# Another order for the first four tiles of an adaLN block: the second tile's k in two parts, two quarters of w_mod straight to TensorE, four more low parts by DMA

## The chip, the cores and the metric

One core of one Trainium2 chip runs the kernel. The engines are TensorE (PE, with its weight loads PEld), VectorE (DVE), ScalarE (ACT), GpSimd (POOL) and SyncE (SP), which here only issues DMAs. Each engine works through its own list of instructions in order and waits on semaphores for what the others make. The metric is the device time of one execution in microseconds (us); the smaller, the better.

## The reference

A block on 2048 tokens of 448 channels, all in float32. Six vectors of modulation come from `c`; two residual branches follow, a linear attention over 16 heads of 28 channels and an MLP across the tokens:

```python
mod = (_silu(c) @ w_mod).reshape(c.shape[0], 6, 1, -1)     # sa, ca, ga, sb, cb, gb
h = _layernorm(x, axis=-1) * (1 + ca) + sa
x = x + ga * _A_ref(h, A_wqkv, A_wo)      # phi(q), phi(k): where(t > 0, t + 1, exp(t)) + 1e-6
h = _layernorm(x, axis=-1) * (1 + cb) + sb
x = x + gb * _B_ref(h, B_w1, B_b1, B_w2, B_b2)   # layernorm, w1 over tokens, gelu, w2 over tokens
```

The attention is linear: kv is the sum over all tokens of the outer product of phi(k) and v, z the sum of phi(k), and each token's output is phi(q) kv / (phi(q) z), then `wo`.

## The kernel before, in words

**Precision.** PE multiplies quickly in the format float32r. An operand is cut into a high part (a copy to float32r, on ACT) and a low part (full minus high), and a product takes three matmuls: high by high, high by low, low by high. The cut `split` (lines 78 to 80) has ACT write the high part and DVE subtract. In a second way (`w_low_dma`, and `split_to` for pieces listed in `PIECE_DMA`) ACT writes the negated high part and a DMA issued by POOL adds the full operand to it in memory.

**Tiles.** The 2048 tokens are 16 tiles of 128 rows. 448 channels are four chunks of 128, where the fourth chunk holds the last 64 channels twice, so that high and low part go through one matmul. A projection (`project`, lines 333 to 347) of one tile onto k or q is 11 matmuls. Tile 0 is the exception: `project0` multiplies the raw float32 weights in 4 slower matmuls, so that it needs no split weights.

**The front (lines 495 to 577).** The order is written out by hand, engine by engine; what an engine meets first in this list it does first. `load_mod` brings four quarters of w_mod for each modulation vector. `mod_acc` (ACT) scales the first quarter by silu(c), `mod_add` (DVE) adds quarters 1, 2 and 3. `col_sum(j)` sums the rows with small matmuls against ones, to have scale and bias of tile 0 as columns: for the first two chunks it takes the accumulation before its last quarter (`part`) and that last quarter directly against `scb`, ones times silu(c); for the other chunks it takes the complete accumulation. `mod_sum` sums the complete accumulation into all rows, and `mod_out` copies it from PSUM to SBUF on ACT.

For a tile t, `a_stats` (DVE, with a power on POOL) gives mean and deviation, `a_norm_a` and `a_norm_b` (DVE) the modulated layernorm h, `a_dup` (ACT) the doubled last chunk, `a_transpose` (PE) turns h, and `a_split` (ACT, DVE) cuts it into `hh` and `hl`. `w_high` (ACT) and `w_low` (DVE) cut wqkv's chunks into `wh` and `wl`. Then k of tile 0, 1, 2 and q of tile 0, 1, 2 are projected; `a_exp` (ACT) and `a_pk` (DVE) make phi(k), `a_phi_q` phi(q), `a_pk_parts` cuts phi(k), and `a_high` cuts h for the outer product. In the order before, k of tile 1 (`project(1, 1, "kp", True)`, all 11 matmuls) stands ahead of q of tile 0, and the low parts of wqkv's k chunks ahead of tile 2's layernorm.

**The loop (lines 581 to 635).** For t from 3 to 15: k of tile t, transposes of t + 1, the outer product of tile t - 3 (`a_outer`, 11 matmuls into four banks), and at t = 3 and 4 also q of tile t.

**The stage after it (lines 840 to 904).** Iteration i transposes `pn` of tile i (phi(q) over its denominator), multiplies by kv and wo (`b_out`), computes the second layernorm for older tiles, and multiplies 12 matmuls of the first group of w1 for tile i - 5 (`step`). DVE makes `pn` (L729, L737) from a sum that POOL raises by 1e-6 (`den`, L722). At the end of an iteration `split_to(10 + (i + 1) // 2)` cuts the next piece of w1 (128 by 512): pieces 10 to 13 in iterations 1, 3, 5 and 7, pieces 14 to 17 in 9, 11, 13 and 15. The rest of the kernel is the MLP: PE with the remaining pieces of w1, gelu, and w2.

**Buffers.** Eight PSUM banks, 76 slots in SBUF for most tiles; a new tile waits until the readers of the tile before it in the same slot are done.

Of the kernel before, what the change touches and what calls it, by code (L numbers as in the profile page):

```python
# [8 lines left out]
F32 = mybir.dt.float32  # L9
# [5 lines left out]
P = 128  # L15
# [3 lines left out]
G = 112  # L19
# [1 line left out]
DH = 28  # L21
EPS = 1e-5

PIECE_DMA = (14, 15, 16, 17)
PRE_LOAD = {12: 2, 13: 4, 14: 6, 15: 8}
KV_LAG = 3
Q_EARLY = (3, 4)
# [20 lines left out]
def block_kernel(ctx: ExitStack, tc: tile.TileContext, x, wqkv, wo, w1, b1, w2, b2, c, wmod, out):  # L48
# [16 lines left out]
    def slot(name, w=D, dt=F32, parts=P):  # L65
        return slots.tile([parts, w], dt, name=name, tag="slot", padded_shape=[P, 512])
# [92 lines left out]
    def mod_out(j, ps):  # L159
        mods[j] = cst.tile([P, D], F32, name=f"mod{j}")  # L160
        nc.scalar.activation(mods[j], ps[:, :D], AF.Copy, bias=1.0 if j in (1, 4) else 0.0)
# [5 lines left out]

    def mod_add(j, k):
        acc = macc[j]
        if k == 3:  # L170
            part[j] = acc
            macc[j] = slot(f"acc{j}_3", parts=G)
        nc.vector.scalar_tensor_tensor(macc[j], wm[j, k], sc[:, k:k + 1], acc, op0=ALU.mult, op1=ALU.add)

    def mod_part(j, k):
# [33 lines left out]
    def w_low(j, ch):  # L209
        w, r = Whi[j, ch], raw_w[j, ch]  # L210
        if ch < 3:
            Wlo[j, ch] = moving(tslot, f"wl{j}_{ch}")
            nc.vector.tensor_sub(Wlo[j, ch], r, w.bitcast(F32))
        else:
            nc.vector.tensor_sub(w[64:128], r[64:128], w[64:128].bitcast(F32))  # L215

    def w_low_dma(j, ch):
        w, r = Whi[j, ch], raw_w[j, ch]
        if ch < 3:
            Wlo[j, ch] = moving(tslot, f"wl{j}_{ch}")  # L220
            lo, hi = Wlo[j, ch], w
        else:
            lo = hi = w[64:128]
            r = r[64:128]
        nc.scalar.activation(lo, hi.bitcast(F32), AF.Copy, scale=-1.0)
        nc.gpsimd.dma_start(lo, r, accum_op=ALU.add)
# [78 lines left out]
    def a_norm_a(t):  # L305
        h = slot(f"h{t}", 512)
        nc.vector.scalar_tensor_tensor(h[:, :D], X[t], st[t][0], mods[1],
                                       op0=ALU.add if t in ACT_STATS else ALU.subtract, op1=ALU.mult)
        hs[t] = h

    def a_norm_b(t, sa=None):
        h = hs[t]
        nc.vector.scalar_tensor_tensor(h[:, :D], h[:, :D], st.pop(t)[1], mods[0] if sa is None else sa,
                                       op0=ALU.mult, op1=ALU.add)

    def a_dup(t):
        nc.scalar.activation(hs[t][:, D:], hs[t][:, 384:D], AF.Copy)
# [3 lines left out]
    def a_transpose(t):  # L321
        h = hs[t]
        tps[t] = bank(f"tp{t}")
        for ch in range(4):
            nc.tensor.transpose(tps[t][:, ch * P:(ch + 1) * P], h[:, ch * P:(ch + 1) * P], ident)  # L325

    def a_split(t):
# [2 lines left out]
        split(tps.pop(t), hh, hl)  # L330
        heads[t] = (hh, hl)

    def project(t, j, name, late_low=False):
        hh, hl = heads[t]
        ps = bank(f"{name}{t}")
        o = ps[:, :D]
        todo = []
        for ch in range(4):
            a, b = (hh, ch, Whi[j, ch]), (hl, ch, Whi[j, ch])
            todo += [a, b] if ch == 3 else [a, (hh, ch, Wlo[j, ch]), b]  # L340
        if late_low:
            ws = [Wlo[j, ch] for ch in range(3)]
            key = lambda m: 3 if m[1] == 3 else 2 if any(m[2] is w for w in ws) else 0 if m[0] is hh else 1
            todo.sort(key=key)
        for n, (a, ch, b) in enumerate(todo):
            nc.tensor.matmul(o, a[:, ch * P:(ch + 1) * P], b, start=(n == 0), stop=(n == 10))  # L346
        return o
# [3 lines left out]
    def a_exp(t, ps):  # L351
        eks[t] = (slot(f"ek{t}"), slot(f"rk{t}"))
        nc.scalar.activation(eks[t][0], ps, AF.Exp)
        nc.scalar.activation(eks[t][1], ps, AF.Relu)
# [56 lines left out]
    def a_pk(t, ps):  # L411
        pkf[t] = phi_k(t, ps, tslot if t < 2 else slot)
# [30 lines left out]
                nc.tensor.matmul(cacc[ch][:, :D], a[:, s], b, start=(t == 0 and i == 0),  # L443
                                 stop=(t == NT - 1 and i == len(todo) - 1))

    scb = cst.tile([G, 64], F32, name="scb")

    h0t = slot("h0t", 512)
    raw_t = {}
# [7 lines left out]
    def col_sum(j):  # L457
        at = 0 if j else 4

        todo = [(part[j], ones[:G, :64], (0, 1)), (wm[j, 3], scb, (0, 1)), (macc[j], ones[:G, :64], (2, 3))]  # L460
        for n, (a, b, chunks) in enumerate(todo):
            for c in chunks:
                ps = colq if j == 0 and c < 2 else colp
                nc.tensor.matmul(ps[:, 64 * (at + c):64 * (at + c + 1)], a[:, CH[c][0]:CH[c][1]], b,
                                 start=(n == c == 0), stop=True, skip_group_check=True)
        groups = ((0, 0, 2, (0, 1)), (0, 2, 3, (2,)), (64, 3, 4, (3,))) if j == 0 else ((0, 0, 3, ()), (64, 3, 4, ()))
        for p0, c0, c1, mod in groups:
            ps = colq if j == 0 and c0 < 2 else colp
            nc.scalar.activation(cols[p0:, at + c0:at + c1], ps[p0:, 64 * (at + c0):64 * (at + c1 - 1) + 1:64], AF.Copy,
                                 bias=float(j))  # L470
            for ch in mod:
                if j == 0 and ch in MOD_ACT:
                    a_mod(ch)
# [14 lines left out]
    def project0(j, name, between):  # L488
        ps = bank(f"{name}0")
        for ch in range(4):  # L490
            nc.tensor.matmul(ps[:, :D], h0t[:, ch * P:(ch + 1) * P], raw_t[j][ch], start=(ch == 0), stop=(ch == 3))  # L491
            between.get(ch, int)()
        return ps[:, :D]

    raw_t = {j: [raw_w[j, ch] for ch in range(4)] for j in (0, 1)}
    a_stats(0)
    nc.vector.tensor_scalar_mul(scb, ones[:G, :64], sc[:, 3:4])
    mod_acc(1)
    nc.scalar.activation(ones_r, ones, AF.Copy)
    mod_acc(0)  # L500
# [23 lines left out]
    a_stats(2)  # L524
    a_split(1)
    w_high(1, 2)
    w_low(1, 1)
    w_high(1, 3)
    w_high(0, 0)
    w_low_dma(0, 0)  # L530
    w_low(1, 2)
    w_low(1, 3)
    mod_out(0, sap)
    a_norm_a(2)
    kp1 = project(1, 1, "kp", True)
    for ch in range(1, 4):
        w_high(0, ch)
    a_norm_b(2)
    a_dup(2)
    a_exp(0, kp0)  # L540
    w_low(0, 1)
    a_stats(3)
    a_pk(0, kp0)
    qps[0] = project0(0, "qp", {1: lambda: a_transpose(2)})
    a_split(2)
    a_norm_a(3)
    a_exp(1, kp1)
    a_high_act(1)
    a_norm_b(3)
    a_dup(3)  # L550
    w_low(0, 2)
    w_low(0, 3)
    a_stats(4)
    a_norm_a(0)
    a_norm_b(0)
    kp2 = project(2, 1, "kp")
    a_high(0)
    a_pk(1, kp1)
    a_transpose(3)
    qps[1] = project(1, 0, "qp", True)  # L560
    del heads[1]
    a_split(3)
    a_norm_a(4)
    a_norm_b(4)
    a_phi_q(1)
    a_high_low(1)
    a_exp(2, kp2)
    a_pk_parts(0)
    a_pk(2, kp2)
    a_phi_q()  # L570
    a_dup(4)
    a_pk_parts(1)
    a_q(2)
    a_high(2)
    a_stats(5)
    a_high(3)
    a_phi_q()
    load_mod(2)
    wo_sb = []
    late = [t for t in range(KV_LAG, NT) if t not in Q_EARLY]  # L580
    for t in range(3, NT):
        kp = project(t, 1, "kp")
        if t + 1 < NT:
            a_transpose(t + 1)
        a_outer(t - KV_LAG)
        if t in Q_EARLY:
            a_q(t)
        if t == 10:
            mp = mod_sum2(2)
        if t + 1 < NT:  # L590
            a_split(t + 1)
        if t + 2 < NT:
            a_norm_a(t + 2)

        for j, i in MOD_AT.get(t, ()):
            mod_part(j, i)
        if 11 <= t < 15:
            nc.vector.tensor_mul(wo_sb[t - 11], wo_sb[t - 11], mods[2][:G])
        a_exp(t, kp)
        if t + 2 < NT:  # L600
            a_norm_b(t + 2)
        a_pk(t, kp)
        a_phi_q()
        a_pk_parts(t - 1)
        if t + 3 < NT:
            a_stats(t + 3)
        if t + 2 < NT:
            a_dup(t + 2)
        if t == 3:
            a_high(4)  # L610
        if t + 2 < NT:
            a_high(t + 2)
        if t == 10:
            mod_out(2, mp)
        if t + 4 < NT:
            load_x(t + 4)
        if 5 <= t < 9:
            mod_part(2, t - 5)
        if t == 9:
            mod_split(2)  # L620
        if 5 <= t <= 5 + QLATE:
            phi_q_sum(t - 5)
        if t in (10, 11):
            load_mod(14 - t)
        if t == 4:
            for g in range(4):
                w = tslot(f"wo{g}", parts=G)
                nc.sync.dma_start(w, wo[g * G:(g + 1) * G, :])
                wo_sb.append(w)
            load_qkv(2, tslot)  # L630
            b1c = cst.tile([P, NF], F32, name="b1c")
            nc.sync.dma_start(b1c, b1.rearrange("(k p) -> p k", p=P))
            b2c = cst.tile([P, NT], F32, name="b2c")
            nc.sync.dma_start(b2c, b2.rearrange("(k p) -> p k", p=P))
        load_to(PRE_LOAD.get(t, 0))
# [562 lines left out]
```

## Time and profile before

| | us |
|---|---|
| median of 3 runs (lowest, highest) | 441.48 (441.41, 441.74) |
| span of the profiled execution | 440.0 |
| PE busy | 434.6 |
| DVE busy | 367.4 |
| ACT busy | 265.0 |
| POOL busy | 118.4 |

The span runs from the first to the last instruction of one profiled execution; the runs' time has 1.48 us more around it. In a timeline a row is a group of like instructions in order: start, time from the first start to the last end, engine, line, operation, `out<-in` by the names above, count, and in brackets how long the engine sat idle and what ended that. In the chain of work that ended last a row is start, time and what. Matmuls are pipelined: the next starts before the one before it has ended, so start to start is the time that one takes of PE.

### The profile page before, as it was taken

The numbers are of one execution on the slowest core, as the hardware profiler recorded it, in microseconds if no ns is written. First come the engines' busy times: TensorE is split into PE (matmuls) and PEld (weight loads), VectorE is DVE, ScalarE is ACT, GpSimd is POOL, SyncE is SP. The second block draws the span as 40 slices with busy tenths as digits, with TensorE's granted clock in tenths as the row PEclk, the third lists the DMA queues.
The fourth block names the chain that finished last, engine by engine and source line by source line (L and its number), as shares of the span: only waits on it lengthen the run. The fifth ranks groups of instructions, "written<-read, shape, count | busy, mean of one in ns | idle before, by whom it ended". The sixth has DMA issues, their size and how long they took to land.

```text
span 440.0 us, 7266 instructions
## 1 busy us (share of the span) xinstructions
PE 434.6 (99%) x2390; PEld 402.4 (91%) x2390; DVE 367.4 (84%) x795; ACT 265.0 (60%) x566; POOL 118.4 (27%) x192
## 2 busy tenths in 40 slices
PE   8999999999999999999999999999999999999996
PEld 7689999999899999999999999999999999999996
DVE  5997897978899999997469586439999988898894
ACT  3868977755646676777666254236675555655550
POOL 2205675520014456564300000010111320231110
PEclk9999999999999999999999999999999999999999
DMA  8987999993430004222417555476667977986531
GB/s 235 292 225 113 172 198 236 220 254 99 134 85 2 24 25 120 50 51 52 140 60 238 162 162 176 135 192 184 155 150 189 181 168 177 185 165 194 86 52 34
DMA packets 64446, 63.47 MB, mean 144 GB/s; under 512 B 8408, under 2 KB 56728, under 8 KB 64408
## 3 DMA queue, kind: packets, MB, share of 16 engines
q1 hardware_dynamic: 54608, 47.62, 36.6%
q0 software_dynamic: 9792, 15.37, 22.3%
q8 instruction: 19, 0.31, 0.3%
q14 instruction: 19, 0.16, 0.1%
q10 hardware_dynamic: 8, 0.00, 0.0%
HBM read 41.88 MB, written 7.34 MB: 112 GB/s over the span
## 4 chain that ended last, share of the span: by engine, by line
PE 95%; DMA 3%; DVE 1%; SPq 0%; issue 0%; DVEq 0%
PE y L1014 19%; PE up L815 10%; PE up L814 10%; PE up L816 10%; PE y L1015 9%; PE op L764 8%; PE cacc L443 8%; PE qp L346 8%; PE kp L346 7%; DMA wr<-in_A_wqkv_dram 2%; PE tq L744 2%; PE tp L325 1%; DMA wm<-in_w_mod_dram 1%; PE kvb L677 1%; PE qp L491 1%; PE wp L832 1%
## 5 line engine op out<-in xcount | busy, mean ns | idle before, releaser
L815 PE MATMUL up<-h2l,ph 128*128 128x448 f32 x224 | 81.3, 363 | 0.0
L814 PE MATMUL up<-h2h,ph 128*128 128x448 f32 x224 | 81.2, 362 | 0.0
L816 PE MATMUL up<-h2h,pl 128*128 128x448 f32 x224 | 80.7, 360 | 0.0
L974 POOL DMA_DIRECT2D a<-a x16 | 14.1, 965 | 145.9 <-DVE u L931 75.9
L814 PEld LDWEIGHTS up<-h2h,ph 128*128 128x128 f32 x224 | 42.0, 188 | 3.3
L80 DVE TENSOR_TENSOR pl<-pr,ph 128x512 fp32r<-128x512 f32 x52 | 35.1, 685 | 11.5 <-ACT ph L79 8.6
L816 PEld LDWEIGHTS up<-h2h,pl 128*128 128x128 f32 x224 | 41.9, 187 | 3.0
L815 PEld LDWEIGHTS up<-h2l,ph 128*128 128x128 f32 x224 | 42.0, 188 | 2.2
L79 ACT ACTIVATE ph<-pr 128x512 fp32r<-128x512 f32 x52 | 31.6, 628 | 17.8 <-PE up L815 11.8
L1036 ACT ACTIVATE cc<-y 128x448 f32<-128x448 f32 x24 | 13.0, 544 | 22.6 <-PE y L1015 22.6
L443 PE MATMUL cacc<-pkh,xh 128*128 128x448 f32 x64 | 24.3, 379 | 0.0
L443 PE MATMUL cacc<-pkl,xh 128*128 128x448 f32 x64 | 23.2, 363 | 0.0
L764 PE MATMUL op<-oh,pth 128*128 128x448 f32 x60 | 23.0, 383 | 0.0
L346 PE MATMUL kp<-wh,hh 128*128 128x448 f32 x60 | 22.2, 375 | 0.2 <-DVE wh L215 0.2
L1057 POOL DMA_DIRECT2D out_dram<-yt x14 | 12.7, 910 | 34.5 <-DVE yt L1043 25.0
L764 PE MATMUL op<-oh,ptl 128*128 128x448 f32 x60 | 21.7, 362 | 0.0
L346 PE MATMUL qp<-wh,hh 128*128 128x448 f32 x60 | 21.6, 365 | 0.0
L346 PE MATMUL kp<-wh,hl 128*128 128x448 f32 x60 | 21.6, 365 | 0.0
L346 PE MATMUL qp<-wh,hl 128*128 128x448 f32 x60 | 21.4, 362 | 0.0
L722 POOL TENSOR_SCALAR den<-den 128x16 f32<-128x16 f32 x16 | 8.8, 549 | 43.0 <-DVE den L719 43.0
L302 POOL TENSOR_TENSOR rs<-ve,mhalf 128x1 f32<-128x1 f32 x16 | 14.6, 915 | 19.0 <-DVE ve L300 18.1
L931 DVE TENSOR_TENSOR u<-u,mod 128x448 f32<-128x448 f32 x14 | 8.7, 619 | 11.9 <-ACT u L930 11.6
(228 smaller groups left out, 1347.4 us busy)
## 6 DMA issues: line engine op xcount, KB each, us to landing
pr<-in_B_w_dram SPq DMA_DIRECT2D x56, 256.0 KB, 3.1
a<-in_B_w_dram SPq DMA_DIRECT2D x32, 256.0 KB, 4.7
a<-in_B_w_dram SPq DMA_DIRECT2D x32, 192.0 KB, 4.6
wm<-in_w_mod_dram SPq DMA_DIRECT2D x24, 196.0 KB, 4.2
x<-in_A_x_dram SPq DMA_DIRECT2D x16, 224.0 KB, 3.9
out_dram<-x SPq DMA_DIRECT2D x14, 224.0 KB, 2.0
out_dram<-yt POOLq DMA_DIRECT2D x14, 224.0 KB, 4.7
pk<-pk POOLq DMA_DIRECT2D x12, 224.0 KB, 4.6
```

The costliest lines, as they stand in the source:

```text
L79: nc.scalar.activation(hi, full, AF.Copy)
L80: nc.vector.tensor_sub(lo, full, hi.bitcast(F32))
L302: nc.gpsimd.tensor_tensor(rs, ve, mhalf[:, 0:1], op=ALU.pow)
L346: nc.tensor.matmul(o, a[:, ch * P:(ch + 1) * P], b, start=(n == 0), stop=(n == 10))
L443: nc.tensor.matmul(cacc[ch][:, :D], a[:, s], b, start=(t == 0 and i == 0), stop=(t == NT - 1 and i == len(todo) - 1))
L764: nc.tensor.matmul(opb[t][:, :D], a[:, g * P:(g + 1) * P], b, start=(n == 0), stop=(n == len(todo) - 1))
L814: nc.tensor.matmul(ps[:, :D], hi[:, sl], mh, start=first, stop=False)
L815: nc.tensor.matmul(ps[:, :D], hi[:, sl], ml, start=False, stop=False)
L816: nc.tensor.matmul(ps[:, :D], lo[:, sl], mh, start=False, stop=last)
L974: nc.gpsimd.dma_start(w, a, accum_op=ALU.add)
L1014: nc.tensor.matmul(ps[:, :D], h[:, s], w, start=opens and r == r0, stop=False, skip_group_check=True)
L1015: nc.tensor.matmul(ps[:, :HD], l[:, s], wh, start=False, stop=closes and r == PAIRS - 1 - (LAST if (q, m) == (NP - 1, 6) else 0), skip_gro ...
```

## The change

Four things change. `PIECE_DMA` grows from pieces 14 to 17 to pieces 10 to 17: four more pieces of w1 get their low part from ACT and a POOL DMA instead of a DVE subtraction. For modulation vector 0, `part` is the accumulation before quarter 2, and quarters 2 and 3 go directly to TensorE, each against its own scaled ones (`scb` is a pair now): two more column sums. k of tile 1 comes in two calls: the six products with the weights' high parts of chunks 0 to 2 ahead of q of tile 0, the three with their low parts and the two of chunk 3 behind it. And the instructions of the front stand in another order: tile 2's layernorm, which reads `sap` from PSUM, ahead of the low parts of k's chunks; exp and phi(k) of tile 0 behind the third tile's work; k of tile 2 ahead of q of tile 1 and its preparation; part of the high cut and phi(q) of tiles 2 and 3 moved into the loop's first turn.

```diff
-PIECE_DMA = (14, 15, 16, 17)
+PIECE_DMA = tuple(range(10, 18))
...
-        if k == 3:
+        if k == (3 if j else 2):
             part[j] = acc
-            macc[j] = slot(f"acc{j}_3", parts=G)
+            macc[j] = slot(f"acc{j}_{k}", parts=G)
...
+    def products(t, j, late):
+        hh, hl = heads[t]
+        if not late:
+            return [(a, ch, Whi[j, ch]) for a in (hh, hl) for ch in range(3)]
+        return [(hh, ch, Wlo[j, ch]) for ch in range(3)] + [(a, 3, Whi[j, 3]) for a in (hh, hl)]
+
+    def project_some(o, todo, first, last):
+        for n, (a, ch, b) in enumerate(todo):
+            nc.tensor.matmul(o, a[:, ch * P:(ch + 1) * P], b, start=(first and n == 0), stop=(last and n == len(todo) - 1))
...
-    scb = cst.tile([G, 64], F32, name="scb")
+    scb = {k: cst.tile([G, 64], F32, name=f"scb{k}") for k in (2, 3)}
...
-        todo = [(part[j], ones[:G, :64], (0, 1)), (wm[j, 3], scb, (0, 1)), (macc[j], ones[:G, :64], (2, 3))]
+        todo = [(part[j], ones[:G, :64], (0, 1))] + [(wm[j, k], scb[k], (0, 1)) for k in range(3 if j else 2, 4)]
+        todo.append((macc[j], ones[:G, :64], (2, 3)))
...
-    nc.vector.tensor_scalar_mul(scb, ones[:G, :64], sc[:, 3:4])
+    for k in scb:
+        nc.vector.tensor_scalar_mul(scb[k], ones[:G, :64], sc[:, k:k + 1])
...
     a_split(1)
     w_high(1, 2)
-    w_low(1, 1)
     w_high(1, 3)
     w_high(0, 0)
     w_low_dma(0, 0)
+    a_norm_a(2)
+    kp1 = bank("kp1")[:, :D]
+    project_some(kp1, products(1, 1, False), True, False)
+    a_norm_b(2, sap[:, :D])
+    mod_out(0, sap)
+    a_dup(2)
+    w_low(1, 1)
     w_low(1, 2)
     w_low(1, 3)
-    mod_out(0, sap)
-    a_norm_a(2)
-    kp1 = project(1, 1, "kp", True)
     for ch in range(1, 4):
         w_high(0, ch)
-    a_norm_b(2)
-    a_dup(2)
-    a_exp(0, kp0)
+    qps[0] = project0(0, "qp", {1: lambda: a_transpose(2)})
+    project_some(kp1, products(1, 1, True), False, True)
     w_low(0, 1)
     a_stats(3)
-    a_pk(0, kp0)
-    qps[0] = project0(0, "qp", {1: lambda: a_transpose(2)})
     a_split(2)
+    a_exp(0, kp0)
     a_norm_a(3)
-    a_exp(1, kp1)
-    a_high_act(1)
     a_norm_b(3)
     a_dup(3)
+    kp2 = project(2, 1, "kp")
+    a_transpose(3)
+    a_exp(1, kp1)
     w_low(0, 2)
     w_low(0, 3)
+    a_pk(0, kp0)
     a_stats(4)
+    a_split(3)
+    a_pk_parts(0)
+    a_high_act(1)
+    a_phi_q()
+    a_exp(2, kp2)
     a_norm_a(0)
     a_norm_b(0)
-    kp2 = project(2, 1, "kp")
-    a_high(0)
+    a_high_act(0)
+    a_norm_a(4)
+    a_high_low(0)
+    a_norm_b(4)
+    a_dup(4)
     a_pk(1, kp1)
-    a_transpose(3)
     qps[1] = project(1, 0, "qp", True)
     del heads[1]
-    a_split(3)
-    a_norm_a(4)
-    a_norm_b(4)
-    a_phi_q(1)
+    a_phi_q()
     a_high_low(1)
-    a_exp(2, kp2)
-    a_pk_parts(0)
+    a_pk_parts(1)
     a_pk(2, kp2)
-    a_phi_q()
-    a_dup(4)
-    a_pk_parts(1)
     a_q(2)
     a_high(2)
     a_stats(5)
-    a_high(3)
-    a_phi_q()
...
         if t == 3:
+            a_high(3)
             a_high(4)
```

## The prediction

> **What bounds the kernel now.** I read the page first, then the chain of work that ended last, then the timelines of PE, DVE and POOL where the chain shows a piece longer than its kind.
>
> ```profile
> span 440.0 us, 7266 instructions
> PE 434.6 (99%) x2390; PEld 402.4 (91%) x2390; DVE 367.4 (84%) x795; ACT 265.0 (60%) x566; POOL 118.4 (27%) x192
> ```
>
> The span is 440.0 us and the median of the runs 441.48: 1.48 us lie around the span, and I take them as unchanged. PE is busy 99% of the span, so a change in order can win only what PE still loses. The change adds no work to PE but two small column sums. Where PE loses time is read from the chain, where equal pieces should take equal times:
>
> ```profile
> 18.24 0.67 PE kp L346 x2
> 18.91 1.50 PE qp L491 x4
> 20.42 0.44 PE tp L325 x4
> 20.85 1.51 PE qp L491 x4
> 22.36 2.21 PE kp L346 x11
> ...
> 25.01 4.42 PE qp L346 x22
> 29.42 2.47 PE kp L346 x11
> 31.89 0.44 PE tp L325 x4
> 32.33 2.27 PE cacc L443 x11
> 34.60 2.20 PE qp L346 x11
> ...
> 43.86 2.20 PE kp L346 x11
> ...
> 166.91 0.58 PE tq L744 x4
> ...
> 197.40 0.63 PE tq L744 x4
> ```
>
> Eleven products take 2.20 to 2.21, so 0.20 each; the fourth tile's k (29.42) takes 0.26 more, the first outer product (32.33) 0.06 more. Four transposes take 0.44; those at 166.91 and 197.40 take 0.14 and 0.19 more. The largest loss lies where this part of the chain begins:
>
> ```profile
> 10.41 0.66 PE L464 MATMUL colq<-ones,acc 112*128 112x64 f32 x4 [0.42 <-DVE acc L173]
> 10.91 0.61 PE L464 MATMUL colq<-scb,wm 112*128 112x64 f32 x4
> 11.35 0.61 PE L464 MATMUL colp<-ones,acc 112*128 112x64 f32 x4
> ...
> 12.61 1.67 PE L491 MATMUL kp<-wr,h0t 128*128 128x448 f32 x4
> ...
> 17.27 0.79 PE L346 MATMUL kp<-wl,hh 128*128 128x448 f32 x3
> 18.24 0.47 PE L346 MATMUL kp<-wh,hh 128*128 128x448 f32 x1 [0.18 <-DVE wh L215]
> 18.55 0.36 PE L346 MATMUL kp<-wh,hl 128*128 128x448 f32 x1
> ```
>
> The three wl products of the second tile's k start at 17.27 and leave PE free at 17.87. The next starts at 18.24, its successor 0.31 later instead of 0.20: 0.48 lost, waiting for DVE's low part of the last weight chunk (the row names L215). So the early losses are 0.48 + 0.26 + 0.06 = 0.80, the late ones 0.14 + 0.19 = 0.33.
>
> **The change part by part.** The DVE rows that the new order moves:
>
> ```profile
> 8.91 2.19 DVE L173 SCALAR_TENSOR_TENSOR acc<-wm,sc,acc 112x448 f32<-112x448 f32 x3 [0.88 <-DMA wm<-in_w_mod_dram]
> ...
> 15.78 0.68 DVE L80 TENSOR_TENSOR hl<-tp,hh 128x512 fp32r<-128x512 f32 x1
> 16.38 1.15 DVE L213 TENSOR_TENSOR wl<-wr,wh 128x448 fp32r<-128x448 f32 x2
> 17.56 0.62 DVE L215 TENSOR_TENSOR wh<-wr,wh 64x448 fp32r<-64x448 f32 x1
> 18.22 0.69 DVE L307 SCALAR_TENSOR_TENSOR h<-x,mv,mod 128x448 f32<-128x448 f32 x1
> 19.04 0.69 DVE L313 SCALAR_TENSOR_TENSOR h<-h,rs,mod 128x448 f32<-128x448 f32 x1
> 19.64 0.62 DVE L213 TENSOR_TENSOR wl<-wr,wh 128x448 fp32r<-128x448 f32 x1
> ...
> 21.11 0.61 DVE L359 SCALAR_TENSOR_TENSOR pk<-ek,rk 128x448 f32<-128x448 f32 x1
> 21.65 0.68 DVE L80 TENSOR_TENSOR hl<-tp,hh 128x512 fp32r<-128x512 f32 x1
> ```
>
> *Quarters of w_mod.* The sums over chunks 0 and 1 need DVE's accumulation only up to its first add (8.91 + 0.68, about 9.6) instead of the second. PE pays one group more, 0.44 (10.91 to 11.35). PE sat idle for 0.42 before 10.41, so at the latest it is free at 9.99; three groups then end at 11.31. The last group cannot start before the third add is out (8.91 + 2.19 = 11.10, plus the 0.06 between DVE's 18.18 and PE's 18.24), 11.16. It stood at 11.35: k of the first tile starts 0.04 to 0.19 earlier. The second scaled vector of ones is one small DVE instruction in the wait for the same transfers: nothing; uncovered it would be some 0.2.
>
> *Second tile's k in two parts.* The first tile's k and the transposes in it take 3.45 (the pieces at 18.91 to 22.36 have the same shape) from 12.61, to 16.06, so now to 15.87 to 16.02; three hh products bring PE to 16.47 to 16.62. The hl products need DVE's low part of the head (15.78 + 0.68 = 16.46), which does not move: everything ahead of it on DVE stays. I let PE wait for it and pay the 0.11 restart seen between 18.24 and 18.55: 16.52 + 0.11 + 0.60 = 17.23. In the chain's reckoning, which has the next piece 0.16 behind (18.91 for a slot that ends at 18.75), that is 17.39, and q of the first tile starts there instead of at 18.91.
>
> From there the chain's own pieces add up: 1.50 + 0.44 + 1.51 to 20.84; five products of the late part, 1.00, to 21.84; k of the third tile 2.21 to 24.05; transposes 0.44 to 24.49; two q 4.42 to 28.91; k of the fourth tile 2.21 without its wait, to 31.12; transposes to 31.56; outer product 2.21 to 33.77. It was 34.60. **Gain 0.83.**
>
> *What covers it.* DVE: the third tile's normalisation (18.22, 19.04) changes places with three low parts (16.38 to 18.18). It ends near 17.9, and its transposes on PE come at 18.7. The low parts end near 19.6 and are used at 20.7 (0.16 off the chain's 20.84). The next low part then stands at about 19.6, as before. Behind it `pk` (21.11) moves back by several instructions, so the head's low part at 21.65 starts near 21.1 and ends at 21.8. The third product of that k needs it at 22.08: 0.3 of room, the least on DVE. Without it PE waits one for one. The fourth tile's low part then comes about two us before its use, which is where the 0.26 goes.
>
> One covered step is a DMA; ACT is the other engine to watch (timeline of POOL, list of DMA issues with KB and us to landing up to 40 us, timeline of ACT):
>
> ```profile
> 17.68 1.04 POOL L226 DMA_DIRECT2D wl<-wr  x1 [1.19 <-ACT wl L225]
> ...
> xl<-h POOLq DMA_DIRECT2D x2, 192.0 KB, 3.9
> wl<-wr POOLq DMA_DIRECT2D x1, 224.0 KB, 7.3
> ...
> 40.99 0.58 ACT L79 ACTIVATE hh<-tp 128x512 fp32r<-128x512 f32 x1
> ```
>
> The low part of wqkv's first q chunk lands at 17.68 + 7.3 = 25.0. It is used six products into the second tile's q: 24.33 (24.49 less 0.16) + 1.20 = 25.53, with about 0.16 to load: 0.3 to 0.4 of room, where before it had more than a microsecond. ACT gets the third tile's exp and relu of q and the fourth tile's high part and negated copy (about 0.58 each by the row at 40.99) behind the loop's start. The first pair fills a wait for PE; the second comes on top, 1.16. The row at 40.99 hangs on PE's q before it, so 40.99 - 0.83 + 1.16 = 41.3, done at 41.9, and k needs it at 43.86 - 0.83 = 43.0. Covered by 1.1. SP's queue keeps its order; POOL's keeps the layernorms' powers in order and meets one DMA (the fourth tile's cut) later, in the loop's first turn, with its use three tiles on.
>
> *Four more pieces of w1.* Each takes one DVE subtraction away and adds one ACT copy and one POOL DMA (busy time in a stretch, then timelines of DVE and POOL):
>
> ```profile
> 160.00:180.00 20.00, 20.00 (x108) 18.40 (x107) 19.73 (x48) 14.12 (x30) 12.30 (x25) 1.00 0.29 80
> 161.80 0.68 DVE L80 TENSOR_TENSOR pl<-pr,ph 128x512 fp32r<-128x512 f32 x1
> ...
> 173.09 0.95 POOL L257 DMA_DIRECT2D pl<-pr  x1
> ...
> 174.75 0.64 POOL L722 TENSOR_SCALAR den<-den 128x16 f32<-128x16 f32 x1 [0.27 <-DVE den L719]
> ...
> 197.29 0.19 DVE L737 COPY pn<-pn 128x64 f32<-128x64 f32 x1
> ```
>
> In this stage (PE, PEld, DVE, ACT, POOL in the first row) DVE is busy 19.73 of 20: it is bound nearly as tightly as PE, and both late stalls are transposes that wait for its `pn` (the copy at 197.29 ends at 197.48, beside the transposes of 197.40). The subtraction at 161.80, about 0.60 up to DVE's next start, falls away in the iteration before the stall at 166.91. 0.60 is more than 0.14 and 0.19 together, so I take both as gone: **gain 0.33**; 0 if DVE waits for something else there, which keeps the far end. The three earlier pieces I cost at nothing: DVE still had room there. ACT has 6 of 20 us free. POOL's DMA delays what stands behind it by about a microsecond; DMAs of the same kind already run in the later iterations, and there the den instruction (174.75) still waited for DVE, not DVE for POOL.
>
> Sum: 0.83 + 0.33 = 1.16 of the span's 440.0, so 438.8, and 441.48 - 1.16 = **440.3**. Bounds: without the 0.11 restart and with the first tile's earlier start (at most 0.19) in full, 0.30 more, 440.0; with no late gain and the two narrow covers (0.3 each) missed by as much again, 0.6 less in front and 0.33 less behind, 441.25.
>
> **The rivals.** 0.2%, about what a measurement here can tell from no change, is 0.88 us.
>
> *Only the front.* DVE's freed 0.60 ends in a wait on ACT or POOL and the late stalls stay: 441.48 - 0.83 = 440.65, within 0.2%. For it: DVE is in step with both engines there. Against it: the stage's DVE idles for 0.27 in 20 us.
>
> *It does nothing.* The order moves the waits instead of removing them: room of 0.3 in two places, a full ACT. Each of the two may cost 0.3 to 0.5, and what is left of 0.83 is noise: 441.2.
>
> *Slower, by the low part that comes by DMA.* PE stands still until it lands, and nothing can pass it. It now has 0.3 to 0.4 of room. Up to 1.5 late it eats only the gain; from 2.4 late the kernel is slower by 0.2%. If it landed 3.4 later (as much again as its 7.3 exceeds the 3.9 median of the xl transfers nearby), 3.0 would be lost: 441.48 - 1.16 + 3.0 = 443.3. Against it: the same issue, from the same instruction, slightly earlier, and no new transfer beside it.
>
> *Slower, by POOL.* If a piece's DMA held POOL far longer than 0.95 under a full DVE, den behind it would come late. In the iteration of 161.80 it may last about 1.2 before DVE waits, and DVE is about 0.4 ahead of PE after losing its subtraction; past 1.6 each microsecond is PE's, and from 3.3 the kernel is slower by 0.2%. DVE leaves POOL a pause of 0.07 in an iteration of 5 (0.27 in 20); held for a whole iteration, the loss is 3.4: 441.48 - 0.83 + 3.4 = 444.0. Against it: 0.95 in the same stage.
>
> The Trainium skill (SBUF — State Buffer, "SBUF: two separate sides") speaks against this part of the change: GpSimd cannot write a DMA's descriptors while DVE holds the port that the two share; the section after it ("A bandwidth-pool intuition that's wrong (but worth ruling out)") gives about 620 ns alone and 3100 ns beside a DVE copy. By that figure the sum would be 441.48 - 0.83 + 1.5 = 442.15, an estimate; this trace, with 0.95 beside a DVE busy 19.73 of 20, does not show the lock.
>
> **How the numbers follow.** Forecast 0.58; only the front 0.17; nothing 0.10; late DMA 0.09; POOL 0.06. Faster by over 0.2%: 0.58. Within 0.2%: 0.27. Slower: 0.15. The forecast's own range is 439.9 to 440.6. With the next two cases it reaches from 440.0 less 0.07 to 441.25 plus 0.26, by the runs' own spread around their median (441.41 to 441.74): 439.9 to 441.5; the slower cases are left out.
>
> **What would show it.** q of the first tile at about 17.4 in the chain instead of 18.91, with the hl products just behind 16.5; no piece over 2.21 among the k products up to 35 and q of the fourth tile near 33.8; transposes of 0.44 at about 166 and 196.3; POOL's four new DMAs near 0.95 each, and den still waiting for DVE. The prediction is wrong if a k or q product waits for a `wl` or an `hl` between 16 and 32, if the first k of the loop waits for ACT's `hh` near 43, or if the stalls of the `pn` transposes are still there.

## The result and the profile after

The changed kernel takes 440.77 us in the median of 21 runs, the kernel before 441.57 beside it: ratio 0.9983, 95% interval 0.9977 to 0.9988, so 0.75 us faster (0.53 to 1.02). Forecast were 440.3 and a gain of 1.16. The profiled execution's span fell from 440.0 to 439.1.

The page of the changed kernel, busy times, and its chain of work that ended last (start, time, what):

```profile
span 439.1 us, 7288 instructions
PE 433.9 (99%) x2394; PEld 402.4 (92%) x2394; DVE 365.1 (83%) x792; ACT 266.9 (61%) x570; POOL 119.3 (27%) x196
```

```profile
12.51 1.50 PE kp L502 x4
...
17.43 8.12 DMA wl<-wr
25.60 3.48 PE qp L356 x16
29.07 2.20 PE kp L356 x11
...
31.71 2.21 PE cacc L453 x11
33.93 2.20 PE qp L356 x11
...
70.09 2.29 PE cacc L453 x11
...
166.32 0.44 PE tq L758 x4
...
196.68 0.44 PE tq L758 x4
```

The fourth tile's k (29.07) takes 2.20, where it took 2.47; the outer product 2.21, where it took 2.27; both late transposes take 0.44, where they took 0.58 and 0.63. All the losses that the prediction listed are gone. The start of a piece in the chain is 0.16 behind that of the same piece in PE's timeline (12.51 for 12.35), so starts are compared within one of the two. New is the second row: a transfer stands in the chain for 8.12 us, the low part of wqkv's first q chunk. What it costs is seen in PE's timeline of the changed kernel:

```profile
12.35 1.67 PE L502 MATMUL kp<-wr,h0t 128*128 128x448 f32 x4
...
16.41 0.79 PE L341 MATMUL kp<-wh,hl 128*128 128x448 f32 x3
17.04 1.67 PE L502 MATMUL qp<-wr,h0t 128*128 128x448 f32 x4
...
24.75 0.77 PE L356 MATMUL qp<-wh,hl 128*128 128x448 f32 x3
25.60 0.88 PE L356 MATMUL qp<-wl,hh 128*128 128x448 f32 x3
26.31 0.36 PE L356 MATMUL qp<-wh,hh 128*128 128x448 f32 x1
```

Three products at 24.75 and three at 25.35 would end their slots at 25.95; the next stands at 26.31. So 0.36 is lost at the second tile's q: the transfer landed at 17.43 + 8.12 = 25.55, 0.55 later than in the profile before although it was issued 0.25 earlier.

Where the 0.9 of the spans came from: q of the fourth tile stands at 33.93 in the chain instead of 34.60, 0.67. One outer product (70.09) gives 0.08 back. At the transposes of 166.32 the lead is 0.59 (166.91 before); there 0.14 was lost before and is not now, so at 196.68 it is 0.72 (197.40 before), and behind those transposes, where 0.19 was lost before, 0.91.

### The profile page after: what moved, and what is told of

It reads as the page before. It is cut to its first block, busy times and chain, and to the rows that moved or that the text cites. A ratio compares the mean times of both kernels' runs of the same rounds, so it can differ in the third digit from the quotient of the medians.

```text
span 439.1 us, 7288 instructions
## 1 busy us (share of the span) xinstructions
PE 433.9 (99%) x2394; PEld 402.4 (92%) x2394; DVE 365.1 (83%) x792; ACT 266.9 (61%) x570; POOL 119.3 (27%) x196
## 4 chain that ended last, share of the span: by engine, by line
PE 95%; DMA 3%; DVE 1%; ACT 0%; issue 0%; SPq 0%; DVEq 0%
PE y L1028 19%; PE up L829 10%; PE up L828 10%; PE up L830 10%; PE y L1029 9%; PE op L778 8%; PE cacc L453 8%; PE qp L356 7%; PE kp L356 7%; DMA wl<-wr 2%; PE tq L758 2%; PE tp L325 1%; DMA wm<-in_w_mod_dram 1%; PE kvb L691 1%; PE wp L846 1%; PE colp L475 0%
## 5 line engine op out<-in xcount | busy, mean ns | idle before, releaser
L80 DVE TENSOR_TENSOR pl<-pr,ph 128x512 fp32r<-128x512 f32 x48 | 32.3, 686 | 11.5 <-ACT ph L79 8.6
L79 ACT ACTIVATE ph<-pr 128x512 fp32r<-128x512 f32 x48 | 29.1, 627 | 17.8 <-PE up L829 7.4
L453 PE MATMUL cacc<-pkh,xh 128*128 128x448 f32 x64 | 24.3, 379 | 0.0
L356 PE MATMUL qp<-wh,hl 128*128 128x448 f32 x60 | 21.4, 362 | 0.0
L356 PE MATMUL kp<-wh,hl 128*128 128x448 f32 x56 | 20.3, 363 | 0.0
L356 PE MATMUL kp<-wh,hh 128*128 128x448 f32 x56 | 20.2, 362 | 0.0
L763 ACT ACTIVATE pth<-tq 128x512 fp32r<-128x512 f32 (+1 forms) x16 | 9.6, 599 | 15.7 <-PE tq L758 15.6
```

Source lines behind the costliest of these rows:

```text
L79: nc.scalar.activation(hi, full, AF.Copy)
L80: nc.vector.tensor_sub(lo, full, hi.bitcast(F32))
```

## The experiments

The theory after the first comparison: front and back each do what the prediction says, and what is missing from the front is PE's wait for the one transfer. The rivals: the parts disturb each other; or the wait is a chance of one profile and the front's working itself was off.

**Each half alone.** The front without the four pieces, and the four pieces without the front:

```diff
-PIECE_DMA = tuple(range(10, 18))      # in the changed kernel: the front alone
+PIECE_DMA = (14, 15, 16, 17)
...
-PIECE_DMA = (14, 15, 16, 17)          # in the kernel before: the pieces alone
+PIECE_DMA = tuple(range(10, 18))
```

> The changed kernel with pieces 10 to 13 cut on DVE again, so only the front is changed. Theory (front and back win separately; the back's 0.32 comes from the subtraction that DVE loses in iteration 7): the transposes of iterations 9 and 15 wait again, a few tenths in all, the span is 0.3 longer than the changed kernel's 439.1, so about 439.4, the front as in the changed kernel. Rival (the late stalls went because PE came earlier or by luck): no late stall, span 439.1.

> The kernel before with only pieces 10 to 13 cut by ACT and POOL's DMA. Theory: the front as before (the chain's q of the fourth tile near 34.6), the two late stalls gone, span 440.0 - 0.3 = 439.7. Rival (POOL's DMA delays what stands behind it, and the relief only pays with the new front): stalls stay or new ones come, span 440.0 or more.

The front alone took 441.01 (ratio 0.9992, interval 0.9983 to 1.0), the pieces alone 441.18 (0.9994, 0.9985 to 1.0003), the kernel before 441.62 on that chip. Neither half's time is cleanly told from no change; the traces tell them apart. First the chain of the front alone, then that of the pieces alone, then PE's timeline of the pieces alone:

```profile
165.88 0.57 PE tq L758 x4
...
196.36 0.63 PE tq L758 x4
```

```profile
166.90 0.44 PE tq L744 x4
...
197.26 0.44 PE tq L744 x4
```

```profile
18.20 0.47 PE L346 MATMUL kp<-wh,hh 128*128 128x448 f32 x1 [0.18 <-DVE wh L215]
```

With the front alone both late stalls are back at their old size; with the pieces alone they are gone, and the early stall for DVE's low part is there as before. So each part removes its own stalls and leaves the other's: the traces show no disturbance of one by the other. The span of the pieces alone was 439.6, near the 439.7 of its theory. That of the front alone was 438.9 and not 439.4: in that execution the transfer landed at 25.0, PE did not wait for it, and q of the fourth tile stands at 33.57 in the chain, 0.36 earlier than in the changed kernel's profile.

**Two ways to give the transfer room.** Issue it earlier, ahead of the high part of the k weights' last chunk; or use it later, with the three products that read it at the end of that q:

```diff
+    w_high(0, 0)
+    w_low_dma(0, 0)
     w_high(1, 3)
-    w_high(0, 0)
-    w_low_dma(0, 0)
...
-            key = lambda m: 3 if m[1] == 3 else 2 if any(m[2] is w for w in ws) else 0 if m[0] is hh else 1
+            key = lambda m: 2 if m[1] == 3 else 3 if any(m[2] is w for w in ws) else 0 if m[0] is hh else 1
```

> The changed kernel with the high part and the negated copy of wqkv's first q chunk one ACT instruction earlier (ahead of the high part of k's last chunk), so that POOL issues its DMA about 0.47 sooner. Theory (the second tile's q waits 0.36 for that transfer, which landed at 25.55): it lands near 25.1 and the wait at 25.6 is gone or below 0.1; the chain's q of the fourth tile near 33.6 instead of 33.93, span about 438.8. Rival (the landing is set by the transfers queued beside it, not by its issue): it still lands near 25.5 and the span stays 439.1.

> The changed kernel with the products with the low parts placed last in the second tile's q, behind the two of the last chunk, so that the late transfer is used 0.40 later; nothing else moves. Theory: landing near 25.5 as in the changed kernel, the wait of 0.36 down to 0 to 0.1, span about 438.8. Rival (the 0.36 is slack that a later wait takes back, for instance the outer products or the loop's first k waiting for ACT): q of the fourth tile earlier, but the span stays at 439.1.

> The changed kernel with both edits of the two runs before: the low part of wqkv's first q chunk is cut and sent ahead of the k weights' last chunk (some 0.5 us earlier), and the three products that read it come last in the second tile's q (0.4 us later). Theory, that the gain of the front missing from the forecast is PE's wait for this transfer in part of the executions: about 0.9 us more room than in the changed kernel, so no wait at these products in the profiled execution, median 440.4 to 440.6, and the runs above 441.2, of which the changed kernel has some, become rare. Rival, that one of the two edits alone is all that can be had and the remaining spread comes from the loads at the start: the same median as with one edit (440.55) and runs up to 441.7 as before.

Issued earlier: 440.56 (0.9980, 0.9971 to 0.9988). Used later: 440.54 (0.9977, 0.9966 to 0.9988). Both: 440.71 (0.9975, 0.9966 to 0.9983). All three overlap the changed kernel's interval, so these times tell none of them from it. In the traces the transfer came at quite different times. Issued earlier, by 0.38 (17.05), it landed at 24.1, 1.4 earlier than in the changed kernel, and PE did not wait; the span was the 438.8 of the theory. Used later, it was issued at 17.92 and took 8.5; it landed at 26.4, and PE still waited, by its timeline:

```profile
26.02 0.37 PE L356 MATMUL qp<-wh,hl 128*128 128x448 f32 x1
26.42 0.88 PE L356 MATMUL qp<-wl,hh 128*128 128x448 f32 x3
27.13 0.36 PE L356 MATMUL qp<-wh,hh 128*128 128x448 f32 x1
```

Four products of 0.20 would have taken 26.02 to 26.82; it is 27.13, so 0.31 lost. The theory of this run missed on all counts: the landing was not near 25.5, the wait not under 0.1, and the span was 439.7 instead of 438.8. Besides the wait, k of the first tile began 0.49 later than in the changed kernel's profile (13.00 for 12.51 in the chain), and one outer product, at 70.52, took 2.48 instead of 2.21. With both it was issued at 17.22, landed at 23.9 and was used at 26.05, without a wait. The median of 440.71 is a miss of the expected 440.4 to 440.6; that runs above 441.2 became rare is right (the highest of 11 is 441.11).

**No transfer at all.** DVE subtracts this low part (0.62), as it does the others, and the fifth tile's second step of normalisation stands one place earlier on DVE; beside it the changed kernel again on the same chip, with a second profile:

```diff
-    w_low_dma(0, 0)
...
+    w_low(0, 0)
     w_low(0, 2)
...
-    a_high_low(0)
     a_norm_b(4)
+    a_high_low(0)
```

> The changed kernel with that low part subtracted by DVE (0.62 us) ahead of its next low part, without the DMA; the fifth tile's second step of normalisation stands one place earlier on DVE. Theory, that only the transfer was late: no wait between 24 and 26 us on PE, because DVE has the low part ready before 24, median 440.4 to 440.6. Rival, that DVE has no room in the front either (0.3 us at the third tile's low part): the head's low part or phi(k) comes 0.6 us later and PE waits for it, 0.3 to 0.6 us at the fourth tile's k or at the first outer product, median 440.9 to 441.2.

> The changed kernel once more, beside the same kernel without the transfer, and a second profile of it. Theory: its k of the first tile starts anywhere between 12.3 and 12.9 us, as the loads come in, and the wait at the three products that read the DMA's low part goes by its landing: 0 where it lands before 25.2, and the rest one for one; from k of the first tile to the attention's kv products it takes 95.5 us plus that wait (95.5 in the runs without a wait, 95.9 with one of 0.36). Median 440.6 to 440.9. Rival: the wait of the first profile was a chance and has no share in the median: the same median as the kernel without the transfer, within 0.1.

> The same kernel as two runs before (first q low part subtracted by DVE, no transfer), on the same chip as the changed kernel. Theory: no wait at those products, 95.5 us from k of the first tile to the kv products whatever the loads do, median 0.1 to 0.3 below the changed kernel's. Rival: the same median as the changed kernel within 0.1.

Without the transfer: 440.55 (0.9977, 0.9967 to 0.9986) and, again, 440.58 (0.9976, 0.9967 to 0.9985). The changed kernel again: 440.85 (0.9984, 0.9975 to 0.9993). Twice the median without the transfer is 0.2 to 0.3 below that of the changed kernel, though only the second was taken beside the changed kernel; there its 11 runs lie within 440.16 to 440.80, the changed kernel's within 440.35 to 441.49. The intervals against the kernel before still overlap, so the size is known to a few tenths only. DVE has room for the subtraction; the rival's waits at the fourth tile's k and the outer product do not appear. The chains of the changed kernel's second profile and of the second profile without the transfer:

```profile
12.47 1.50 PE kp L502 x4
...
24.23 4.41 PE qp L356 x22
28.64 2.21 PE kp L356 x11
30.84 0.44 PE tp L325 x4
31.28 2.21 PE cacc L453 x11
33.49 2.20 PE qp L356 x11
```

```profile
12.34 1.50 PE kp L502 x4
...
24.09 4.42 PE qp L356 x22
28.50 2.20 PE kp L356 x11
30.71 0.44 PE tp L325 x4
31.14 2.21 PE cacc L453 x11
33.35 2.20 PE qp L356 x11
```

From k of the first tile to q of the fourth these take 33.49 - 12.47 = 21.02 and 33.35 - 12.34 = 21.01; the first profile of the changed kernel took 33.93 - 12.51 = 21.42. In its second profile the transfer took 6.7, landed at 24.1, and PE did not wait. So the wait of 0.36 is not in every execution: it depends on when the transfer lands. Two more profiles have the transfer and its use as in the changed kernel: the front alone (landed at 25.0, no wait) and the kernel without the third quarter below (25.35, 0.03 lost).

The first profile without the transfer has a span of 439.2 in spite of that, because k of its first tile starts at 13.08 in the chain, 0.74 later than in the second profile of the same kernel; from there to q of the fourth tile it takes 21.08.

**What the landing depends on.** Only the DMA's issue is moved, behind POOL's power for the fourth tile; ACT's copy stays:

```diff
+        if (j, ch) == (0, 0):
+            return lambda: nc.gpsimd.dma_start(lo, r, accum_op=ALU.add)
         nc.gpsimd.dma_start(lo, r, accum_op=ALU.add)
...
-    w_low_dma(0, 0)
+    send_wl = w_low_dma(0, 0)
...
     w_low(0, 1)
     a_stats(3)
+    send_wl()
```

> The changed kernel with the POOL DMA of wqkv's first q low part issued 4.2 us later, behind POOL's power for the fourth tile (21.06 to 21.62 us); ACT's negated copy stays where it is. Theory, that PE stands still for this transfer one for one once its room is gone: it lands 7 to 8 us after an issue at 21.65, at 28.7 to 29.7, PE waits 3.0 to 4.3 us before the second tile's q (less the 0.36 that the changed kernel lost there in its profile), and nothing gives it back: median 443.4 to 444.7. Rival, that the transfer takes that long because it queues behind the loads of the start, so that a later issue lands nearly at the same time (26 to 27): a wait of 1 to 1.7, median 441.4 to 442.1. A second rival, that later slack takes part of the wait up: the wait in the trace and the difference of the times disagree by over 1 us.

Measured: 441.09 (0.9985, 0.9976 to 0.9994), not the 443.4 to 444.7 of the theory, and below the 441.4 to 442.1 of the first rival too. POOL's timeline, the list of DMA issues (KB each, us to landing) and PE's timeline of this kernel:

```profile
21.42 1.04 POOL L227 DMA_DIRECT2D wl<-wr  x1
```

```profile
wl<-wr POOLq DMA_DIRECT2D x1, 224.0 KB, 4.2
```

```profile
24.67 0.77 PE L358 MATMUL qp<-wh,hl 128*128 128x448 f32 x3
25.65 0.88 PE L358 MATMUL qp<-wl,hh 128*128 128x448 f32 x3 [0.22 <-DMA wl<-wr]
26.37 0.36 PE L358 MATMUL qp<-wh,hh 128*128 128x448 f32 x1
```

Issued 4.0 later than in the changed kernel, the transfer landed at 25.6, as it did there. PE lost 26.37 - 24.67 - 1.20 = 0.50, less than the rival's 1 to 1.7. The first rival holds in its main point: the time to landing is no duration that can be added to an issue. What the transfer may stand in line with is seen in the DMA engines' share (the last but one column; the last is GB/s) of three profiles: the changed kernel's first and second, and the one with the late issue.

```profile
20.00:22.00 2.00, 2.00 (x10) 1.61 (x9) 1.93 (x6) 1.12 (x3) 0.56 (x1) 1.00 1.09 267
...
23.00:24.00 1.00, 1.00 (x8) 0.89 (x7) 0.97 (x2) 1.00 (x3) 0.00 (x0) 1.00 0.94 181
24.00:25.00 1.00, 1.00 (x8) 0.94 (x7) 0.97 (x3) 0.77 (x3) 0.00 (x0) 1.00 0.11 13
...
25.00:25.50 0.50, 0.50 (x3) 0.14 (x1) 0.47 (x2) 0.50 (x2) 0.00 (x0) 1.00 0.00 0
```

```profile
22.00:23.00 1.00, 1.00 (x6) 0.94 (x6) 1.00 (x2) 0.34 (x2) 0.00 (x0) 1.00 0.85 151
23.00:24.00 1.00, 1.00 (x9) 0.90 (x8) 0.94 (x3) 0.79 (x2) 0.00 (x0) 1.00 0.15 26
```

```profile
22.00:23.00 1.00, 1.00 (x6) 0.94 (x5) 0.93 (x2) 0.21 (x2) 0.46 (x1) 1.00 0.60 163
23.00:24.00 1.00, 1.00 (x9) 0.90 (x7) 0.94 (x3) 0.91 (x3) 0.00 (x0) 1.00 1.11 194
24.00:25.00 1.00, 1.00 (x7) 0.94 (x6) 1.00 (x2) 0.75 (x2) 0.00 (x0) 1.00 0.36 66
```

The share is near 1 for most of this stretch (0.60 in one microsecond of the last) and then falls: as an estimate from these rows, the full load ends at about 23.9 in the changed kernel (landing 25.55), at about 23.0 in its second profile (24.1), at about 24.3 with the late issue (25.6). That the transfer waits among the loads of the start is inferred from this; no run takes loads away. The Trainium skill (DMA: Bandwidth & Descriptors, "Issuing engines are not separate DMA queues") says that DMAs of all issuing engines run on the same 16 DMA engines and interleave there; these rows fit that, but do not tell the transfer from the loads. The same page's fit for one DMA that POOL issues ("Anatomy of one DMA — SWDGE (gpsimd) path", 2.0 us plus bytes over 436 GB/s) would give an estimate of 2.5 us for 224 KB; measured here are 4.2 to 8.5, and the measurement decides.

The end of the loads is not all of it. In the changed kernel the engines move nothing from 25.0 to 25.5, and the transfer lands only at 25.55: the last part of its time is not spent in line for the engines. Over the profiles the landing trails that end by 0.2 (both edits) to 2.4 (used later). Issues at 17.05 and 17.22 landed at 24.1 and 23.9, issues between 17.4 and 18.1 anywhere from 24.0 to 26.4, the one at 21.4 at 25.6. Whether the earlier issue helps a little, or those two were lucky executions, isn't settled by one profile each.

**The other two parts of the front.** The third quarter of w_mod accumulated by DVE as before; and k of the second tile in one piece ahead of q of the first, with all else in the new order:

```diff
-        if k == (3 if j else 2):          # the quarter back on DVE; with it go its scaled ones and its column sums
+        if k == 3:
...
-    kp1 = bank("kp1")[:, :D]              # k in one piece
-    project_some(kp1, products(1, 1, False), True, False)
...
+    kp1 = project(1, 1, "kp", True)
     qps[0] = project0(0, "qp", {1: lambda: a_transpose(2)})
-    project_some(kp1, products(1, 1, True), False, True)
```

> The changed kernel with w_mod's third quarter accumulated by DVE as before and not sent to TensorE. Theory: k of the first tile starts 0.1 to 0.2 us later; the second tile's part of k then starts as much later, and as its low part of the head follows from transposes inside that k, little of it is hidden: median 0.0 to 0.2 above the changed kernel's, 440.8 to 441.0. Rival, that the quarter was a main part of the front's gain: 0.4 us or more above, 441.2.

> The changed kernel with k of the second tile in one piece ahead of q of the first, as in the kernel before, all else in the new order. Theory, that the split is what makes the new order of DVE's work possible: the weights' low parts end at about 20.0 us there, so the second tile's k ends at about 20.5 and q of the first tile starts at 20.2 to 20.6 instead of 17.04; PE loses 1.5 to 2.0 us of it for good, median 442.2 to 442.9. Rival, that the order of the rest gives the gain and the split is dispensable: within 0.4 us of the changed kernel, at most 441.2.

Without the quarter: 440.81 (0.9979, 0.9970 to 0.9988), no difference that these runs can tell. Its first tile's k starts at 12.47 in PE's timeline; with the quarter it starts at 12.2 to 13.0 in the other profiles of the new order, and in the two profiles of the kernel without the transfer at 12.91 and 12.18. This spread is several times the 0.04 to 0.19 in question, so the quarter's own share is not shown.

In one piece: 442.40 (1.0017, 1.0008 to 1.0027), 0.77 slower than the kernel before on its chip. PE's timeline:

```profile
18.96 1.01 PE L356 MATMUL kp<-wl,hh 128*128 128x448 f32 x2 [0.84 <-DVE wl L213]
20.15 0.47 PE L356 MATMUL kp<-wh,hh 128*128 128x448 f32 x1 [0.18 <-DVE wh L215]
20.46 0.36 PE L356 MATMUL kp<-wh,hl 128*128 128x448 f32 x1
20.66 1.66 PE L502 MATMUL qp<-wr,h0t 128*128 128x448 f32 x4
```

PE stands still for the low parts that DVE now makes behind the third tile's layernorm, and q of the first tile starts at 20.66 instead of 17.04. The new order of DVE's work needs the split: without it, it makes the kernel slower. The split in the old order was not run.

## Why the prediction was right, and where it was off

*The side and the mechanism.* Faster, by PE's stalls in the front and two late ones, as forecast. The gain was 0.75 instead of 1.16, and 440.77 lies in the range and 0.47 above the forecast. One of the prediction's own signs of being wrong came true all the same: in the first profile a q product waits for a `wl` between 16 and 32 (25.60).

*Second tile's k in two parts.* Right. q of the first tile was to start at 17.39 in the chain's reckoning; it stands at 17.04, which is 17.20 there. The hl products stand at 16.41, before the forecast 16.52, and lose 0.03 up to q (17.04 - 16.41 - 0.60) instead of the restart of 0.11. On DVE the head's low part, "which does not move", did move:

```profile
8.73 2.17 DVE L173 SCALAR_TENSOR_TENSOR acc<-wm,sc,acc 112x448 f32<-112x448 f32 x3 [0.45 <-DMA wm<-in_w_mod_dram]
...
15.59 0.68 DVE L80 TENSOR_TENSOR hl<-tp,hh 128x512 fp32r<-128x512 f32 x1
```

Its place in DVE's order is the same, but the whole run in front of it began 0.18 earlier (8.73 for 8.91), by the row as a load of w_mod came in, and it came 0.19 earlier (15.59 for 15.78) with it. The new order needs the split: by the two ratios to the kernel before (1.0017 and 0.9983) the kernel without it is 1.5 us above the changed kernel.

*Quarters of w_mod.* The first tile's k started 0.26 earlier (12.35 for 12.61) instead of 0.04 to 0.19, but a kernel without this part took a time that these runs cannot tell from it, and that k's start moves by more than this between executions: no gain of the quarter is shown.

*The covers.* DVE's (the head's low part, 0.3 of room) and ACT's (1.1) held; no wait for either appears. The transfer's did not, and this is the step that cost most: "The low part of wqkv's first q chunk lands at 17.68 + 7.3 = 25.0 ... 0.3 to 0.4 of room". It took 7.3 for the transfer's own duration, to be added to any issue. The runs show a landing that does not follow the issue, between 23.9 and 26.4 in the profiles, against a need of about 25.3 (26.1 before): room that is there in some executions and not in others. The rival "Slower, by the low part that comes by DMA" named the right mechanism with a far too large end (3.4 later), because it scaled a duration that is none; against it the prediction set an issue that is "slightly earlier", which is no argument when the issue does not set the landing.

*The front's sum.* Without this wait the forecast holds. From k of the first tile to q of the fourth the kernel before takes 34.60 - 12.77 = 21.83 (its k stands at 12.61, 12.77 in the chain's reckoning); the two executions without a wait shown above take 21.01 and 21.02, the five others with none above 0.03 take 21.07 to 21.10. In four of these five the early products of the second tile's k are longer than 1.20, as in the chain of the front alone:

```profile
15.92 1.28 PE kp L341 x6
```

There the head's low part ends about 0.1 ahead of its use (15.58 + 0.68 = 16.26 for a product at 16.36 in the front alone), so part of the forecast's 0.11 is paid in some executions. From that k on the gain is 0.73 to 0.82. The forecast's 0.83 held 0.04 to 0.19 for that k's earlier start, so 0.64 to 0.79 of it lay here: this part came out at or a little above it. The changed kernel's first profile has 21.42, so 0.41, and 0.26 from the earlier start.

*Four more pieces of w1.* Right: 0.33 forecast; the stalls of 0.14 and 0.19 are gone, with the pieces and only with them. The three earlier pieces cost nothing that the chain shows: from q of the fourth tile to the transposes of 166.90 the kernel with the pieces alone takes 132.33, the kernel before 132.31. The rival "Slower, by POOL" is off by POOL's timeline of the changed kernel, in the iteration that lost its subtraction:

```profile
161.91 0.97 POOL L257 DMA_DIRECT2D pl<-pr  x1
...
163.57 0.65 POOL L736 TENSOR_SCALAR den<-den 128x16 f32<-128x16 f32 x1 [0.24 <-DVE den L733]
```

The DMA holds POOL for 0.97, and den still waits 0.24 for DVE: 1.21 in all, as much as the prediction allowed before DVE would wait. In this stage DVE is busy 19.73 of 20 us, as before. The lock figure of 3100 ns (the Trainium skill, SBUF — State Buffer, "A bandwidth-pool intuition that's wrong (but worth ruling out)") is not shown here either.

*The missing part of the sum.* 1.16 less 0.75 is 0.41. The transfer accounts for a part: 0.36 in one profile, 0 in another, 0.2 to 0.3 by the medians of the version without it, whose ratio of 0.9976 is 1.06 us. The rest, 0.1 to 0.2, is within the intervals and stays open. One candidate is in the loop: in three of the eleven profiles of the new order an outer product takes 2.29 (70.09), 2.48 (70.52, used later) and 2.40 (89.86, with both edits) instead of 2.21. What it waits for is not shown.

## What to carry to other kernels

The time from issue to landing in a busy stretch is not a duration that can be added to another issue time: read when the DMA engines run out of earlier work, count room from there, and allow for a spread over executions (24.1 and 25.55 in two profiles of the changed kernel; 23.9 to 26.4 over all kernels here). Where an engine has 0.6 us to spare, computing a small operand on it can be safer than a transfer that must arrive within a few tenths. And an order of work and the split that makes it possible are one change: here the order without the split was as much slower than the kernel before as the whole change was faster.

## What was not expected of the hardware

A DMA that POOL issued 4.0 us later landed at the same time (25.6 for 25.55), in 4.2 us instead of 8.1. Why a landing trails the end of the full load by 0.2 us in one execution and by 2.4 in another, in some with engines that move nothing just before it, is open. The start of the first tile's k moved between 12.2 and 13.0 us over profiles of kernels of the new order. In two executions of the kernel without the transfer it was 12.91 and 12.18, and their times (on two chips) were 440.92 and 440.16: the spread of the start is as large as the gain of the whole change, and sets what a comparison here can tell.
